# The second batch's keys: pooled by GpSimd and transposed on TensorE, in place of pooling by small matmuls

## The chip, the cores and the metric

The kernel runs on one core of one Trainium2 chip. A core has five engines with a queue each: TensorE (PE, with its weight loads as PEld), VectorE (DVE), ScalarE (ACT), GpSimd (POOL) and SyncE (SP, which here issues transfers). The metric is the time of one execution on the device in microseconds. Before the change it is 291.39 us in the median of 7 runs (290.43 to 291.57).

## What is computed

Attention with pooled keys and values, then a feed-forward layer with the activation h cos h. There are 8 batches, 8 heads, 576 positions and 64 dimensions for each head; keys and values are averaged over groups of 8 positions, so each head has 72 pooled keys.

```python
def _attn_ref(q, k, v):
    B, H, S, D = q.shape            # 8, 8, 576, 64
    pool = 8
    Sp = S // pool                  # 72
    scale = 1.0 / np.sqrt(D)
    k_p = k.reshape(B, H, Sp, pool, D).mean(axis=3)
    v_p = v.reshape(B, H, Sp, pool, D).mean(axis=3)
    scores = scale * np.matmul(q, k_p.transpose(0, 1, 3, 2))
    scores = scores - np.max(scores, axis=-1, keepdims=True)
    attn = np.exp(scores)
    attn = attn / (np.sum(attn, axis=-1, keepdims=True) + 1e-09)
    return np.matmul(attn, v_p)

def _moe_ref(x, w_in, w_out):       # x: 4608 x 512, w_in: 512 x 2048, w_out: 2048 x 512
    h = x @ w_in
    g = h * np.cos(h)
    return g @ w_out
```

All tensors are float32 in memory; the kernel works in bf16 with float32 sums.

## The kernel before

The feed-forward layer is done in 9 tiles of 512 tokens, `t` = 0 to 8; attention is done a batch (576 tokens) at a time. A prologue computes the attention of batch 0. In tile `t` PE first does the **up phase**, eight pairs `fp` of 128-column blocks, each pair 8 matmuls of 128x512 (L317); ACT takes the cosine (L327) and DVE the product (L331). Then comes the **down phase**, into which the attention of batch `t + 1` is woven. Tile 0 does the down phase with 64 plain matmuls of 128x512 (L334), numbered `n` = 0 to 63; later tiles use a scheme of seven half-size products (L395). The order in every queue is the order of the program text: the kernel is scheduled by hand, each engine runs its instructions in that order, and semaphores make an instruction wait for what it needs.

**Tile 0.** Its attention is that of batch 1. Its keys come in an "even" layout, 128 partitions each holding 9 successive positions of a head, so the pooling over 8 positions crosses partitions. `pool_k_mm` (L168) does it on PE: a matmul with a 0/1 matrix `groups` adds the positions and transposes in one step, 36 small matmuls for two pairs of heads. It is called twice after the up pair `fp` = 4, into the banks `obanks`; `put_kk` (L143) copies the sums to `kk[1]` with four copies on DVE and four on ACT. After `fp` = 5 and 6, `q_transpose_mm` (L203) transposes the queries of batch 1 on PE, nine blocks of 128x128 each time.

In the down phase of tile 0 a list `fill` says before which `n` a piece of attention goes: the rest of batch 0 (`scores(t, REST)`, L222), the first scores of batch 1 (`S_(0, 0)`), the pooling of the values by matmuls (`pool_v_mm`, L176), the products with the values (L251, `V_`). The matmuls run over w_out's pieces in the order 0, 2, 1, 3: `n` = 8 is the first that needs piece 2, `n` = 16 piece 1, `n` = 24 piece 3.

**Later batches.** `load_kv` (L114) loads keys or values with 72 partitions, each holding the 8 positions of one pooled key. `pool_add` does the pooling on POOL: four adds of halves (L151), two more (L153), and for keys two (L156) that write the sum twice side by side into `kp2`. `k_transpose` (L182) moves `kp2` to `kk` by a transposing transfer.

**Loads.** POOL issues all loads of tile 0 in one row: q, k and v of batch 0, w_in pieces 0 to 2, the keys of batch 1 (`load_even`, L95), half of its queries, w_in 3, the other queries, w_out 0, the values of batch 1; three memsets (`vz[1]`, `kp2`); w_out 2, 1 and 3 (L128); then keys, queries and values of batch 2. POOL's transfers count on eight semaphores in rotation: an issue waits until the transfer eight places before it has landed. The issue of the values of batch 2 also waits for `pool_v_mm` on PE, whose input it overwrites. Then POOL computes four weight differences (L351) and pools the keys and values of batch 2.

PSUM has three double banks `banks[0..2]` and two single ones, `obanks`. `g1` to `g4` are SBUF tiles for later tiles; before these, g1 and g2 hold scratch with which DVE builds `groups` in the first 4 us, and g3 holds `groups`.

Of the kernel before, what the change touches and what calls it, by code (L numbers as in the profile page):

```python
# [10 lines left out]
BF16 = mybir.dt.bfloat16  # L11
ACTF = mybir.ActivationFunctionType
ADD = mybir.AluOpType.add
SUB = mybir.AluOpType.subtract

POOL = 8
# [4 lines left out]
def kernel(  # L21
# [9 lines left out]
    nc = tc.nc  # L31
    B, H, S, D = q.shape
    Sp = S // POOL
# [37 lines left out]
    g1, g2, g3, g4 = [wpool.tile([128, HF, HT], BF16, name=f"g{i}") for i in range(1, 5)]  # L71
# [4 lines left out]
    kk = [wpool.tile([128, H, SpA], BF16, name=f"kk{i}") for i in range(2)]  # L76
    kp2 = [wpool.tile([SpA, H, 2, D], BF16, name=f"kp2{i}") for i in range(2)]
# [16 lines left out]
    def load_even(dst, b, src, j0=0, j1=KCH):  # L94
        nc.gpsimd.dma_start(out=dst[:, j0:j1].rearrange("p j t d -> p j (t d)"), in_=even_view(src, b, j0, j1))  # L95
# [31 lines left out]
    def load_w_out(cg):  # L127
        nc.gpsimd.dma_start(  # L128
            out=w_out_sb[cg],
            in_=moe_w_out[cg * 512:(cg + 1) * 512, :].rearrange("(f p) m -> p f m", p=128))  # L130
# [14 lines left out]
    def pool_add(b, which):  # L145

        st = staged.pop((which, b))
        x, s = st, half_sums
        add = nc.gpsimd.tensor_tensor
        for h in range(0, H, 2):  # L150
            add(out=s[:, h:h + 2], in0=x[:, h:h + 2, 0:4, :], in1=x[:, h:h + 2, 4:8, :], op=ADD)  # L151
        for h in range(0, H, 4):
            add(out=s[:, h:h + 4, 0:2, :], in0=s[:, h:h + 4, 0:2, :], in1=s[:, h:h + 4, 2:4, :], op=ADD)  # L153
        if which == "k":
            for slot in range(2):
                add(out=kp2[b % 2][:Sp, :, slot, :], in0=s[:, :, 0, :], in1=s[:, :, 1, :], op=ADD)  # L156
        else:
            s = s.rearrange("p (j a) t d -> p j a t d", a=2)
            add(out=v_part(b), in0=s[..., 0, :], in1=s[..., 1, :], op=ADD)
# [12 lines left out]
    def pool_v_mm(b, pair):  # L172
        vb = staged["v", b]
        for t in range(ROW):
            for hp, rows in enumerate(half):
                nc.tensor.matmul(pair[:Sp, hp, 0:KCH * D], lhsT=groups[rows, t, :], rhs=vb[rows, :, t, :],  # L176
                                 start=(t == 0), stop=(t == ROW - 1))
        nc.vector.tensor_copy(out=v_part(b).rearrange("p j a d -> p a j d"),
                              in_=pair[:Sp, :, 0:KCH * D].rearrange("p a (j d) -> p a j d", j=KCH))

    def k_transpose(b):
        nc.sync.dma_start_transpose(out=kk[b % 2], in_=kp2[b % 2].rearrange("p h s d -> p (h s d)"))  # L182
# [290 lines left out]
    q_tile(1)  # L473
    for cg in range(3):
        load_w_in(cg)
    load_even(staged["k", 1], 1, k)
    load_even(staged["q", 1], 1, q, 0, 2)
    load_w_in(3)
    load_even(staged["q", 1], 1, q, 2, 4)
# [2 lines left out]
    nc.gpsimd.memset(vz[1], float(POOL))  # L482
    for i in range(2):
        nc.gpsimd.memset(kp2[i], 0.0)
    for cg in (2, 1, 3):
        load_w_out(cg)

    def warm_up(n, bank):

# [34 lines left out]
    for t in range(NT):  # L524
        b = t + 1
        if t > 0:

            for fp in up_order(t)[0:2]:
                up_mm(t, fp, 0, 2)
        for n, fp in enumerate(up_order(t)):  # L530
            up_mm(t, fp, 2 if n < 2 else 0)
            between = ()
            if t == 0:
                if fp == 4:
                    puts = pool_k_mm(1, obanks[0], 0, 2), pool_k_mm(1, obanks[1], 2, 4)
                elif fp in (5, 6):
                    g0 = 9 * (fp - 5)
                    puts = q_transpose_mm(1, obanks[0], g0, g0 + 5), q_transpose_mm(1, obanks[1], g0 + 5, g0 + 9)
                if fp in (4, 5, 6):
                    puts[0](vec)  # L540
                    between = ((puts[1], act),)
            up_g(t, fp, between)
            if 0 < t and 3 <= n < 6:
                put_gs(*[(k, 0) for k in (((3,), (1,), ()) if t == 1 else ((1, 2), (3,), (4,)))[n - 3]])
            if 0 < t and b < B:
                if n == 0:
                    q_transpose(b)
                elif n == 2:
                    k_transpose(b)
        mms = [(ms, fc) for ms in range(4) for fc in range(FFCH)]  # L550
        if t == 0:
            mms = [(ms, fc) for hm in range(2) for cg in (0, 2, 1, 3) for ms in range(2 * hm, 2 * hm + 2)
                   for fc in range(4 * cg, 4 * cg + 4)]


        def S_(n, bank):
            return lambda: scores(b, us[n], banks[bank])

        later = []

        def V_(n, bank, wait=None):
            return lambda: values(b, us[n], banks[bank], wait)

        fill = []
        if t < B:
            exp_tables()
            fill = [(1, lambda: scores(t, REST, banks[2])), (16, lambda: values(t, REST, banks[1]))]
        if t == 0:
            fill = [(2, fill[0][1]), (2, S_(0, 0)), (8, lambda: pool_v_mm(1, banks[1])),
                    (8, lambda: values(t, REST, banks[2])), (8, S_(1, 0)), (8, V_(0, 1)),  # L570
                    (18, S_(2, 2)), (21, V_(1, 0, later)), (26, S_(3, 1)), (32, lambda: later.pop()()),
                    (32, V_(2, 2)), (40, V_(3, 0))]
        if t < FIRST:
            fi = 0
            for n, (ms, fc) in enumerate(mms):
                while fi < len(fill) and fill[fi][0] <= n:
                    fill[fi][1]()
                    fi += 1
                down_mm(obanks[ms % 2], ms, fc)
                if fc == FFCH - 1:  # L580
                    down_out(t, ms, obanks[ms % 2])
                if n == 4:
                    put_weights(0, nc.vector, (1,))
                elif n == 36:
                    put_weights(1, nc.vector, (3,))
            put_weights(1, nc.vector, (2, 4))
        else:
            products, reads = down_products(t)

            def product(i, j=0, k=2 * HF):  # L590
                for mm in products[i][j:k]:
                    mm()

            us = BY_TOKENS
            later = []

            u0, u1, u2, u3 = [(b, us[i], banks[j]) for i, j in enumerate((2, 1, 0, 1))]
            ur = (t, REST, banks[2])

            def scores_of(*parts):  # L600
                for part in parts:
                    scores_mm(*part)
                for part in parts:
                    scores_exp(*part)

            def muls():
                while later:
                    later.pop(0)()

            steady, rest = b < B, t < B  # L610
            if rest:
                exp_tables()
            product(0)
            product(1, 0, 2)
            if steady:
                scores_of(u0, u1, u2)
            elif rest:
                scores_of(ur)
            product(1, 2)
            if t == 1:  # L620
                put_g(2, 0)
            put_gs((1, 1), (2, 1))
            reads[0]()
            put_g(3, 1)
            reads[1]()
            if t == 1:
                put_g(4, 0)
            if steady:
                values(*u0, later)
            product(2)  # L630
            reads[2]()
            muls()
            if steady:
                values(*u1, later)
            product(3)
            reads[3]()
            muls()
            put_g(4, 1)
            if steady:
                values(*u2, later)  # L640
            product(4)
            reads[4]()
            muls()
            if steady:
                scores_of(ur, u3)
            product(5, 0, 4)
            if rest:
                values(*ur, later)
            product(5, 4, 12)
            muls()  # L650
            if steady:
                values(*u3, later)
            product(5, 12)
            reads[5]()
            muls()
            product(6)
            reads[6]()
        if t < B:
            sin_tables()
        if 0 < t and b + 1 < B:  # L660

            nc.gpsimd.tensor_copy(out=gate, in_=kk[b % 2][0:1, 0, 0:1])
        if b + 1 < B:
            load_kv(b + 1, "k", k)
            load_q(b + 1)
            load_kv(b + 1, "v", v)
            if t == 0:
                put_weights(0, nc.gpsimd, (3, 2, 4))
                put_weights(1, nc.gpsimd, (1,))
            pool_add(b + 1, "k")  # L670
            pool_add(b + 1, "v")
# [28 lines left out]
```

The softmax here doesn't subtract the row's maximum and nothing guards it: scores larger than these inputs give would overflow.

## Time and profile before

| | |
|---|---|
| median of 7 runs | 291.39 us (290.43 to 291.57) |
| the profiled execution | 291.24 us |
| its span, first to last instruction | 289.5 us |
| PE busy | 280.7 us (97%) |
| DVE busy | 233.5 us (81%) |
| ACT busy | 207.9 us (72%) |
| POOL busy | 150.9 us (52%) |
| mean clock granted to PE | 0.997 of full |
| mean of all transfers | 114 GB/s |
| transfers from 20 to 45 us | 204 to 207 GB/s |

The span is what the profiler sees of one execution, so its parts are compared with each other and with the span; the medians of several runs are compared with each other. Busy time is a sum over the whole span; where the change acts, from 7 to 45 us, the timeline of each engine has to be read.

### The profile page before, as it was taken

Reading aid. Unit: us, or ns where it says so; the run is one execution under the profiler, and the core shown is the slowest. Engines: PE = TensorE matmul, PEld = TensorE weight load, DVE = VectorE, ACT = ScalarE, POOL = GpSimd, SP = SyncE. Lnnn points to the kernel's source line nnn. Section 1 sums busy time; section 2 is a strip of 40 time slices with the busy share of each in tenths; the row PEclk is TensorE's granted clock in tenths of the full one; section 3 lists DMA queues with packets and bytes.
Section 4 is the critical chain, followed back from the end, with each engine's and each line's share of the span. In section 5 each row is a group of like instructions: output and inputs, shape, how many; then the busy total and the mean of one; then the engine's idle time right before and its main releaser. Section 6 shows DMA issues by size and latency. Waiting matters only on the chain.

```text
span 289.5 us, 5446 instructions
## 1 busy us (share of the span) xinstructions
PE 280.7 (97%) x2168; PEld 178.0 (62%) x2168; DVE 233.5 (81%) x314; ACT 207.9 (72%) x265; POOL 150.9 (52%) x145
## 2 busy tenths in 40 slices
PE   7889999999999999999999999999999999999994
PEld 2545554446864586458745884588448854884583
DVE  6458747799988989798989897989798979855972
ACT  3786798378887798679966997699759976436600
POOL 8553189995698469836984499439920000000000
PEclk9999999999999999999999999999999999999998
DMA  7999999454939592969185936694670060006014
GB/s 155 203 207 207 206 205 213 111 109 60 174 77 177 72 163 43 204 87 165 24 188 82 176 51 151 106 170 71 146 106 0 5 144 1 2 7 140 0 39 109
DMA packets 44489, 32.97 MB, mean 114 GB/s; under 512 B 22192, under 2 KB 40112, under 8 KB 44464
## 3 DMA queue, kind: packets, MB, share of 16 engines
q0 software_dynamic: 19744, 18.07, 40.0%
q1 hardware_dynamic: 24080, 14.03, 23.6%
q10 hardware_dynamic: 640, 0.52, 0.8%
q8 instruction: 17, 0.28, 0.4%
q14 instruction: 8, 0.07, 0.1%
HBM read 36.70 MB, written 9.44 MB: 159 GB/s over the span
## 4 chain that ended last, share of the span: by engine, by line
PE 67%; DVE 6%; ACT 0%; issue 0%; DVEq 0%
PE obank L395 29%; PE bank L317 26%; PE bank L251 4%; PE obank L317 4%; PE bank L222 2%; DVE g_sb L331 2%; PE bank L395 2%; DVE xT L262 2%; DVE g L361 2%; DVE o_two L411 1%; ACT cos L327 0%; DVE q_sb L411 0%; DVEq L411 0%
## 5 line engine op out<-in xcount | busy, mean ns | idle before, releaser
L317 PE MATMUL bank<-xT,w_in_sb 128*128 128x512 bf16 x512 | 114.0, 379 | 0.1
L327 ACT ACTIVATE cos<-bank,half_pi 128x1024 f32<-128x1024 f32 x64 | 70.3, 1113 | 46.8 <-PE bank L317 46.8
L317 PEld LDWEIGHTS <-w_in_sb 128*128 128x128 bf16 x576 | 56.1, 98 | 66.1 <-issue 0.5
L331 DVE TENSOR_TENSOR g_sb<-bank,cos 128x1024 bf16<-128x1024 f32 x64 | 77.2, 1220 | 21.0 <-ACT cos L327 21.0
L151 POOL TENSOR_TENSOR half_sums<-kv_st 72x512 f32<-72x512 bf16 x48 | 54.3, 1158 | 27.1 <-DMA kv_st<-in_k_dram 26.6
L395 PEld LDWEIGHTS <-g 128*128 128x128 bf16 x512 | 48.9, 98 | 7.2 <-issue 1.4
L262 DVE TENSOR_TENSOR xT<-bank,inv 64x512 bf16<-64x512 f32 (+1 forms) x72 | 45.3, 629 | 6.3 <-ACT inv L258 4.9
L257 ACT ACTIVATE inv<-bank 64x512 f32<-64x512 f32 (+1 forms) x72 | 39.1, 544 | 10.5 <-PE bank L251 9.4
L395 PE MATMUL obank<-w,g 128*128 128x256 bf16 x368 | 43.6, 272 | 0.0
L395 PEld LDWEIGHTS <-g_sb 128*128 128x128 bf16 x384 | 36.8, 98 | 7.8 <-issue 1.2
L229 ACT ACTIVATE ex<-bank 72x1024 bf16<-72x1024 f32 (+1 forms) x40 | 35.0, 928 | 2.0 <-PE bank L222 1.9
L153 POOL TENSOR_TENSOR half_sums<-half_sums 72x512 f32<-72x512 f32 x24 | 32.2, 1359 | 0.0
L395 PE MATMUL obank<-w_out_sb,g_sb 128*128 128x256 bf16 x240 | 28.9, 273 | 0.3 <-DVE g_sb L331 0.3
L361 DVE TENSOR_TENSOR g<-g_sb 128x1024 bf16<-128x1024 bf16 x32 | 23.6, 736 | 0.5
L258 ACT ACTIVATE inv<-inv 128x512 f32<-128x512 f32 (+1 forms) x36 | 21.0, 583 | 1.1
L251 PE MATMUL bank<-ex,vz 72*128 72x256 bf16 (+1 forms) x176 | 20.0, 243 | 0.1
L156 POOL TENSOR_TENSOR kp<-half_sums 72x512 bf16<-72x512 f32 x12 | 16.3, 1374 | 0.5
L251 PEld LDWEIGHTS <-vz 72*128 72x128 bf16 x176 | 13.6, 97 | 3.5 <-DVE xT L262 0.5
L334 PE MATMUL obank<-w_out_sb,g_sb 128*128 128x512 bf16 x64 | 15.3, 379 | 0.4 <-DMA w_out_sb<-in_moe_w_out_dram 0.4
L395 PE MATMUL obank<-w_out_sb,g 128*128 128x256 bf16 x112 | 15.7, 273 | 0.0
L395 PE MATMUL obank<-w,g_sb 128*128 128x256 bf16 x128 | 15.3, 273 | 0.0
L317 PE MATMUL obank<-xT,w_in_sb 128*128 128x512 bf16 x64 | 15.1, 379 | 0.0
(85 smaller groups left out, 246.4 us busy)
## 6 DMA issues: line engine op xcount, KB each, us to landing
out_dram<-o_two SPq DMA_DIRECT2D x64, 128.0 KB, 2.4
kv_st<-in_v_dram POOLq DMA_DIRECT2D x8, 576.0 KB, 12.8
kv_st<-in_k_dram POOLq DMA_DIRECT2D x7, 576.0 KB, 7.7
q_b<-in_q_dram POOLq DMA_DIRECT2D x6, 576.0 KB, 10.0
w_in_sb<-in_moe_w_in_dram POOLq DMA_DIRECT2D x4, 512.0 KB, 14.4
w_out_sb<-in_moe_w_out_dram POOLq DMA_DIRECT2D x4, 512.0 KB, 18.3
q_b<-in_q_dram POOLq DMA_DIRECT2D x4, 288.0 KB, 12.7
g_sb<-in_k_dram SPq DMA_DIRECT2D x1, 576.0 KB, 3.6
```

The lines of the kernel that those rows point to most:

```text
L151: add(out=s[:, h:h + 2], in0=x[:, h:h + 2, 0:4, :], in1=x[:, h:h + 2, 4:8, :], op=ADD)
L153: add(out=s[:, h:h + 4, 0:2, :], in0=s[:, h:h + 4, 0:2, :], in1=s[:, h:h + 4, 2:4, :], op=ADD)
L229: nc.scalar.activation(out=ex[:, 0:nh * n].rearrange("p (a n) -> p a n", a=2), in_=pair[:Sp, :, 0:nh * n // 2], func=ACTF.Exp, scale=scale ...
L251: nc.tensor.matmul(pair[:, hp, (i // 2) * n:(i // 2 + 1) * n], lhsT=vz[b % 2][:, pj, 2 * hp:2 * hp + 2, :].rearrange("p a d -> p (a d)"), ...
L257: nc.scalar.activation(out=inv[half[1 - hp]], in_=pair[half[1 - hp], hp, 0:w], func=ACTF.Ln)
L258: nc.scalar.activation(out=inv, in_=inv, func=ACTF.Exp, scale=-1.0)
L262: nc.vector.tensor_mul(out=x_out(b, u, half[hp]), in0=cols(pair[half[hp], hp, :], u), in1=cols(inv[half[1 - hp]], u))
L317: nc.tensor.matmul(h[j] if h is obanks else h[:, j, :], lhsT=w_in_sb[fc // 4][:, ki, (fc % 4) * 128:(fc % 4 + 1) * 128], rhs=xT[:, ki, t * ...
L327: nc.scalar.activation(out=c, in_=ps, func=ACTF.Sin, bias=half_pi[:, :1])
L331: nc.vector.tensor_mul(out=o, in0=ps, in1=c)
L361: nc.vector.tensor_tensor(out=out[:, f0:f1], in0=x, in1=y, op=op)
L395: mms.append(lambda bank=bank, first=first, g=g, w=w, fc=fc, p=p: nc.tensor.matmul(bank[p], lhsT=g(fc, p), rhs=w(fc), start=(first and fc ...
```

## The change

The keys of batch 1 are no longer loaded in the even layout. They are loaded as later batches are, with 72 partitions, in two halves of four heads into `g1` and `g2`, which are free by then. `pool_add` learns to take its input from two parts. It is called for batch 1 on POOL after the issue of w_out pieces 2 and 1, ahead of piece 3. The two calls of `pool_k_mm` in the up phase of tile 0 and their copies are gone. A new function `k_transpose_mm` transposes the sums on PE, a head at a time, into `banks[2]`, and DVE copies them to `kk[1]` in one instruction; it is called at the end of the up phase, ahead of the first down matmul. The first two entries of `fill` go from `n` = 2 to `n` = 4.

```diff
     def pool_add(b, which):
 
         st = staged.pop((which, b))
-        x, s = st, half_sums
+        parts = st if isinstance(st, list) else [st]
+        s = half_sums
         add = nc.gpsimd.tensor_tensor
         for h in range(0, H, 2):
-            add(out=s[:, h:h + 2], in0=x[:, h:h + 2, 0:4, :], in1=x[:, h:h + 2, 4:8, :], op=ADD)
+            i, h0 = divmod(h, H // len(parts))
+            x = parts[i][:, h0:h0 + 2]
+            add(out=s[:, h:h + 2], in0=x[:, :, 0:4, :], in1=x[:, :, 4:8, :], op=ADD)
...
+    def k_transpose_mm(b, bank):
+        ps = bank.bitcast(BF16)[:, 0:H * Sp].rearrange("p (h n) -> p h n", n=Sp)
+        for h in range(H):
+            nc.tensor.matmul(ps[:, h, :], kp2[b % 2][:Sp, h].rearrange("p s d -> p (s d)"), identity[:Sp, :Sp],
+                             is_transpose=True)
+        nc.vector.tensor_copy(out=kk[b % 2][:, :, 0:Sp], in_=ps)
...
     for cg in range(3):
         load_w_in(cg)
-    load_even(staged["k", 1], 1, k)
+    staged["k", 1] = [x[:Sp].rearrange("p f n -> p (f n)").rearrange("p (h t d) -> p h t d", h=H // 2, t=POOL)
+                      for x in (g1, g2)]
+    for i, x in enumerate(staged["k", 1]):
+        nc.gpsimd.dma_start(out=x.rearrange("p h t d -> p h (t d)"),
+                            in_=k[1, 4 * i:4 * i + 4].rearrange("h (p t) d -> p h (t d)", t=POOL))
     load_even(staged["q", 1], 1, q, 0, 2)
...
-    for cg in (2, 1, 3):
+    for cg in (2, 1):
         load_w_out(cg)
+    pool_add(1, "k")
+    load_w_out(3)
...
             if t == 0:
-                if fp == 4:
-                    puts = pool_k_mm(1, obanks[0], 0, 2), pool_k_mm(1, obanks[1], 2, 4)
-                elif fp in (5, 6):
+                if fp in (5, 6):
                     g0 = 9 * (fp - 5)
                     puts = q_transpose_mm(1, obanks[0], g0, g0 + 5), q_transpose_mm(1, obanks[1], g0 + 5, g0 + 9)
-                if fp in (4, 5, 6):
                     puts[0](vec)
                     between = ((puts[1], act),)
...
         if t == 0:
+            k_transpose_mm(1, banks[2][:, 0, :])
             mms = [(ms, fc) for hm in range(2) for cg in (0, 2, 1, 3) for ms in range(2 * hm, 2 * hm + 2)
                    for fc in range(4 * cg, 4 * cg + 4)]
...
-            fill = [(2, fill[0][1]), (2, S_(0, 0)), (8, lambda: pool_v_mm(1, banks[1])),
+            fill = [(4, fill[0][1]), (4, S_(0, 0)), (8, lambda: pool_v_mm(1, banks[1])),
```

## The prediction

> **What bounds the kernel now.** I read the page first: TensorE (PE) is busy 97% of the 289.5 us span, and the chain that ended last is 67% PE. A PE microsecond won or lost should therefore reach the end, unless a wait stands in its way. All edits lie before 45 us, so I went to the timeline of that stretch, engine by engine. First PE (start us, us, engine, line, operation, shapes, count, idle before and its releaser):
>
> ```profile
> 25.86 1.36 PE L168 MATMUL obank<-g,kv_st 64*64 64x72 bf16 x72
> 27.15 1.90 PE L317 MATMUL bank<-xT,w_in_sb 128*128 128x512 bf16 x8
> 28.89 0.67 PE L203 MATMUL obank<-identity,q_b 128*128 128x128 bf16 x9
> 29.39 1.89 PE L317 MATMUL bank<-xT,w_in_sb 128*128 128x512 bf16 x8
> 31.11 0.67 PE L203 MATMUL obank<-identity,q_b 128*128 128x128 bf16 x9
> 31.62 1.89 PE L317 MATMUL bank<-xT,w_in_sb 128*128 128x512 bf16 x8
> 33.34 0.59 PE L334 MATMUL obank<-w_out_sb,g_sb 128*128 128x512 bf16 x2
> 33.87 0.55 PE L222 MATMUL bank<-qT,kk 64*72 64x64 bf16 x12
> 34.35 1.47 PE L334 MATMUL obank<-w_out_sb,g_sb 128*128 128x512 bf16 x6
> 35.97 1.17 PE L176 MATMUL bank<-kv_st,g 64*72 64x256 bf16 x18
> 38.44 1.89 PE L334 MATMUL obank<-w_out_sb,g_sb 128*128 128x512 bf16 x8
> 40.70 0.59 PE L334 MATMUL obank<-w_out_sb,g_sb 128*128 128x512 bf16 x2 [0.36 <-DMA w_out_sb<-in_moe_w_out_dram]
> ```
>
> The first line is what the change removes: 72 small matmuls, worth 27.15 - 25.86 = 1.29 us from start to next start. The last line matters most: the 17th down matmul (n=16) starts at 40.70 because it waited for the third piece of w_out. PE was there about 0.5 us earlier (38.44 + 8 x 0.2205, the pace of L317 and L334 from start to start, is 40.20). So time won before 40.7 us is not all kept. From 40.70 to the end of this down phase at 53.5 PE shows no idle; a shift of n=16 is a shift of the end.
>
> Then GpSimd (POOL), which gets the new work:
>
> ```profile
> 17.09 0.74 POOL L95 DMA_DIRECT2D kv_st<-in_v_dram  x1 [2.86 <-DMA w_in_sb<-in_moe_w_in_dram]
> 17.82 0.97 POOL L482 MEMSET vz<- 72x1024 bf16 x1
> 18.71 1.86 POOL L484 MEMSET kp<- 80x1024 bf16 x2
> 20.50 0.75 POOL L128 DMA_DIRECT2D w_out_sb<-in_moe_w_out_dram  x1
> 22.21 0.74 POOL L128 DMA_DIRECT2D w_out_sb<-in_moe_w_out_dram  x1 [0.96 <-DMA w_in_sb<-in_moe_w_in_dram]
> 37.44 0.84 POOL L114 DMA_DIRECT2D kv_st<-in_v_dram  x1 [7.61 <-PE bank L176]
> 74.70 4.50 POOL L151 TENSOR_TENSOR half_sums<-kv_st 72x512 f32<-72x512 bf16 x4 [5.18 <-DMA kv_st<-in_k_dram]
> 79.16 2.94 POOL L153 TENSOR_TENSOR half_sums<-half_sums 72x512 f32<-72x512 f32 x2
> 82.18 2.50 POOL L156 TENSOR_TENSOR kp<-half_sums 72x512 bf16<-72x512 f32 x2
> ```
>
> POOL issues its loads over eight semaphores in rotation, so a load waits until the one eight places before it has landed. It is idle 7.61 us before 37.44. The last three lines are one pooling of keys as it stands later in the kernel: the same eight adds that the change puts into the first up phase.
>
> [...]the adds of L153 take 1.26 us at the median, but 1.72 at most. Between 24 and 34 us DVE runs only L331 (one PSUM input) and copies out of PSUM, so I expect the short times. [...]here nine take 29.39 - 28.89 = 0.50 us in a row, 55 ns each, and I use that.[...]
>
> **Part by part.**
>
> *Removed.* 1.29 us of PE at 25.86; four DVE casts (1.26 us) and four ACT casts (1.13 us), which lay beside PE and which no matmul waited for: worth nothing.
>
> *The key load.* It becomes two loads of 72 partitions into g1 and g2, still before q and w_in 3: the same bytes at the same place in the queue. g1 and g2 are free (DVE's last read of them ends at 3.7 us). [...]The landing of each later load is set by its slowest engine: one runs about 1.5 to 2 us late in the trace. [...]the last landing comes some 0.4 us earlier (w_in 3 at 28.8 becomes about 28.2, w_out's third piece at 40.65 about 40.3). If not, up to 0.8 later.
>
> *One load more on the semaphores.* All later issues move back a place in the rotation: v of batch 1 waits for w_in 1 (landed 19.41 by issue plus time to landing) instead of w_in 0. An issue came 0.28 us after its landing for w_out 0, v and w_out 3, so v goes out at 19.69 instead of 17.09, a shift of 2.6. The queue is full until past 40 us (DMA share at its ceiling, 207 GB/s), so transfers don't start later. But POOL's own order does: memsets and two w_out issues follow as before (20.50 - 17.09 = 3.41, then 0.75 and 0.74), giving 19.69 + 3.41 + 1.49 = 24.60 as the start of pooling. Both key halves are there by about 24.
>
> *The pooling.* L151 and L153 run 7.03 us where nothing disturbs them (4.49 + 2.50 and a gap), L156 2.50: 9.53 us. It ends at 24.60 + 9.53 = 34.13. It was hidden in POOL's idle 7.61 us as to POOL; w_out 3 goes out at 34.2 instead of 25.0, still before the queue runs dry, so it costs nothing. Upper bound: the pooling at 46.88 us took 10.88, with DVE's two-input subtractions beside it: end 35.5. Lower bound: the shortest rows with no gaps, 4.49 + 2.49 + 2.50 = 9.48.
>
> *PE's path.* The sixth pair of up matmuls now starts at 25.86 and ends at 27.60; nine transposes to 28.10; then w_in 3, about 0.3 us of wait; two more groups of eight and nine transposes (1.74 + 0.50 + 1.72): the up phase ends at about 32.3 instead of 33.34. The new transposes wait for kp2 there: with about 0.1 us of signal they start at 34.2. PE stands idle 1.9 us, and everything queued behind it on PE, the whole down phase, stands too. Eight transposes at 55 ns are 0.42. Then four down matmuls (0.88) to 35.5. The rest scores reuse the bank that DVE's new copy reads. DVE is free of the last up product at about 34.9 (PE end 32.3 + 0.2 + cosine 1.11 + product 1.23), and the copy of 576 columns costs about 0.45 (128x640 took 0.49)[...]: done at 35.4 to 35.7. So the scores start at 35.5 to 35.7. From there to n=16, by before's intervals: scores 0.48, four matmuls 0.88, pooling of v 1.10, its copy to the first values 0.92, values 0.45, eight matmuls 1.77 = 5.60. n=16 starts at 41.1 to 41.3 instead of 40.70. The wait for w_out is gone; what is late in its place is kp2. Sum: +0.4 to +0.6 us.
>
> *Later.* v of batch 2 is issued after the pooling of v1 on PE, about 0.7 us later, and POOL's weights and poolings with it. POOL waits 2.4 us and more at its gate in later tiles, and kp2 for batch 2 (57.8) is asked for at 60.0: no cost.
>
> Profiled execution: 291.24 us, span 289.5, so 1.7 outside the span; the median of the runs is 291.39, 0.15 above it. I add the change to the median.
>
> **Rivals.**
> - A, likeliest (0.55): PE waits for kp2 as worked out; +0.3 to +1.0, my value +0.6 because small delays on this chain only add: 292.0.
> - B (0.15): POOL is disturbed and pools in 10.9 us: transposes at 35.6, n=16 at 42.5, +1.8: 293.2. For it: the first pooling of the trace took that. Against: no two-input DVE work here.
> - C, not slower (0.25): kp2 is in time. The matmuls removed less the transposes added are 0.87 us of PE, and the last wait is again w_out's third piece, at about 40.3: 0.4 earlier, 291.0; up to 0.9 if w_out comes earlier too. It decides if pooling ends by about 33.3, that is 0.8 earlier than my sum: possible only if the issue of v doesn't wait for w_in 1's slowest engine, or the adds run shorter than any in the trace. Against: every term is a measured row.
> - D (0.05): the idle 1.9 us together with the wait for w_in 3 lets PE's clock fall[...].
>
> **Numbers.** 292.0, range 290.9 to 293.3: A whole, most of B and C. About 0.6 us (0.2%) is what a measurement of this kernel tells from none. A gives 0.25 within and 0.30 slower; B and D 0.20 slower; C 0.13 faster, 0.12 within: faster 0.13, same 0.37, slower 0.50.
>
> **What would show it.** Right: eight adds on POOL from about 24.6 to 34.1; a PE gap of 1.5 to 2.2 us before the new transposes, released by POOL; no wait on w_out at n=16, which starts near 41.2; from there the old distances. Wrong: pooling ends before PE comes (no gap, C); a clock under full after 34 us (D); n=16 waiting for w_out later than 40.7[...]; later stages longer than before.

## The result and the profile after

| | before | changed |
|---|---|---|
| median | 291.3 us (32 runs, 290.31 to 291.9) | 293.12 us (13 runs, 291.66 to 293.83) |
| ratio | | 1.0059, 95% interval 1.0046 to 1.0071 |
| profiled execution, its span | 291.24 us, 289.5 us | 293.83 us, 291.9 us |
| PE busy | 280.7 us | 279.9 us |
| POOL busy | 150.9 us | 161.7 us |

The change makes the kernel 0.59% slower, about 1.7 us. PE does 0.8 us less work and POOL 10.8 us more. The profiled execution of the changed kernel is the slowest of its 13, so its trace shows the losses large. I read it for places and causes, and the medians for sizes.

The timeline of PE in the changed kernel (line numbers are those of the changed file: L327 is the up phase, L213 the query transposes, L187 the new transposes, L344 the down phase, L232 the scores, L179 the pooling of v):

```profile
28.26 0.67 PE L213 MATMUL obank<-identity,q_b 128*128 128x128 bf16 x9
29.57 1.90 PE L327 MATMUL bank<-xT,w_in_sb 128*128 128x512 bf16 x8 [0.64 <-DMA w_in_sb<-in_moe_w_in_dram]
31.31 0.67 PE L213 MATMUL obank<-identity,q_b 128*128 128x128 bf16 x9
31.81 1.89 PE L327 MATMUL bank<-xT,w_in_sb 128*128 128x512 bf16 x8
34.76 0.43 PE L187 MATMUL bank<-identity,kp 72*128 72x72 bf16 x8 [1.06 <-POOL kp L159]
35.02 1.03 PE L344 MATMUL obank<-w_out_sb,g_sb 128*128 128x512 bf16 x4
36.53 0.55 PE L232 MATMUL bank<-qT,kk 64*72 64x64 bf16 x12 [0.47 <-DVE kk L189]
...
40.45 2.32 PE L344 MATMUL obank<-w_out_sb,g_sb 128*128 128x512 bf16 x10
...
45.22 0.59 PE L344 MATMUL obank<-w_out_sb,g_sb 128*128 128x512 bf16 x2 [0.27 <-DMA w_out_sb<-in_moe_w_out_dram]
```

The small matmuls are gone, and four waits stand in the brackets of these lines that weren't there: for w_in 3 (0.64), for GpSimd's sums (1.06), for DVE's copy of the transposed sums (0.47), and, at the 25th down matmul, for w_out's fourth piece (0.27). The wait at the 17th, the one that bound before, is gone: n=16 is the ninth of the ten at 40.45, so it starts near 40.45 + 8 x 0.2205 = 42.2, 1.5 us later than before. The next up phase starts at 55.39 instead of 53.48, 1.9 us later. Half a microsecond more is lost in tile 2, where PE waits 0.29 us for a product of DVE; what set that off was not tried.

Part of the lateness is not the change's. The up phase itself started 0.78 us later, because PE had waited longer for the first queries of batch 0, a load issued ahead of everything that the change touches. Before:

```profile
7.49 0.45 PE L203 MATMUL bank<-identity,q_b 128*128 128x128 bf16 x5 [0.58 <-DMA q_b<-in_q_dram]
...
17.10 8.82 PE L317 MATMUL bank<-xT,w_in_sb 128*128 128x512 bf16 x40
```

and in the changed kernel:

```profile
8.21 0.45 PE L213 MATMUL bank<-identity,q_b 128*128 128x128 bf16 x5 [1.33 <-DMA q_b<-in_q_dram]
...
17.88 10.55 PE L327 MATMUL bank<-xT,w_in_sb 128*128 128x512 bf16 x48
```

In the thirteen traces used here this start lies between 16.78 and 17.88 us, and the changed kernel's is the latest. So times of one execution are not sizes of the change.

The timeline of POOL in the changed kernel:

```profile
19.32 0.74 POOL L95 DMA_DIRECT2D kv_st<-in_v_dram  x1 [1.78 <-DMA w_in_sb<-in_moe_w_in_dram]
...
22.97 0.74 POOL L128 DMA_DIRECT2D w_out_sb<-in_moe_w_out_dram  x1 [0.17 <-issue]
24.43 0.74 POOL L128 DMA_DIRECT2D w_out_sb<-in_moe_w_out_dram  x1 [0.72 <-DMA g<-in_k_dram]
25.19 4.49 POOL L154 TENSOR_TENSOR half_sums<-g 72x512 f32<-72x512 bf16 x4
29.65 2.48 POOL L156 TENSOR_TENSOR half_sums<-half_sums 72x512 f32<-72x512 f32 x2
32.21 2.49 POOL L159 TENSOR_TENSOR kp<-half_sums 72x512 bf16<-72x512 f32 x2
34.65 0.78 POOL L128 DMA_DIRECT2D w_out_sb<-in_moe_w_out_dram  x1
```

The pooling takes 32.21 + 2.49 - 25.19 = 9.51 us, as in the undisturbed rows of the trace before. It starts 0.6 us later than forecast, because the issue ahead of it waits until the first key half has landed.

And DVE at the hand-over, where L341 is the product of the last up pair and L189 the new copy:

```profile
34.88 1.22 DVE L341 TENSOR_TENSOR g_sb<-bank,cos 128x1024 bf16<-128x1024 f32 x1 [1.01 <-ACT cos L337]
36.02 0.45 DVE L189 COPY kk<-bank 128x576 bf16<-128x576 bf16 x1
```

The transposes were done at about 35.0; the copy began a microsecond later, when DVE had finished the product. PE had come late to that last pair because of w_in 3, and the copy inherited it.

The loads themselves, each by its issue plus its time to landing: w_in 3 landed at 11.34 + 18.2 = 29.5 us (before: 9.16 + 19.6 = 28.8), w_out's third piece at 24.43 + 17.0 = 41.4 (40.6), its fourth at 34.65 + 10.5 = 45.2 (43.1). The sixteen landing records of w_in 3 stand in two groups now: eight between 26.0 and 26.8, eight between 27.5 and 29.5. Before, fifteen stood between 26.2 and 27.4 and one at 28.8. These too are the times of one slow execution; how they vary is told with the runs on the loads.

### The profile page after: what moved, and what is told of

The parts are those of the page before. It is cut to its first block, busy times and chain, and to the rows that moved or that the text cites. A ratio compares the mean times of both kernels' runs of the same rounds, so it can differ in the third digit from the quotient of the medians.

```text
span 291.9 us, 5324 instructions
## 1 busy us (share of the span) xinstructions
PE 279.9 (96%) x2104; PEld 176.9 (61%) x2104; DVE 233.0 (80%) x311; ACT 206.6 (71%) x261; POOL 161.7 (55%) x154
## 4 chain that ended last, share of the span: by engine, by line
PE 69%; DVE 3%; ACT 0%; issue 0%
PE obank L405 31%; PE bank L327 27%; PE bank L261 4%; PE obank L327 4%; PE bank L232 3%; DVE g_sb L341 2%; PE bank L405 2%; DVE g L371 1%; ACT cos L337 0%; DVE o_two L421 0%
## 5 line engine op out<-in xcount | busy, mean ns | idle before, releaser
L327 PE MATMUL bank<-xT,w_in_sb 128*128 128x512 bf16 x512 | 113.9, 379 | 0.9 <-DMA w_in_sb<-in_moe_w_in_dram 0.6
L327 PEld LDWEIGHTS <-w_in_sb 128*128 128x128 bf16 x576 | 56.2, 98 | 67.3 <-issue 1.2
L341 DVE TENSOR_TENSOR g_sb<-bank,cos 128x1024 bf16<-128x1024 f32 x64 | 77.1, 1219 | 21.0 <-ACT cos L337 20.9
L154 POOL TENSOR_TENSOR half_sums<-kv_st 72x512 f32<-72x512 bf16 x48 | 55.3, 1179 | 28.1 <-DMA kv_st<-in_k_dram 27.6
L267 ACT ACTIVATE inv<-bank 64x512 f32<-64x512 f32 (+1 forms) x72 | 39.2, 544 | 11.8 <-PE bank L261 10.8
L156 POOL TENSOR_TENSOR half_sums<-half_sums 72x512 f32<-72x512 f32 x26 | 34.2, 1332 | 0.0
L371 DVE TENSOR_TENSOR g<-g_sb 128x1024 bf16<-128x1024 bf16 x32 | 23.0, 720 | 0.5
L159 POOL TENSOR_TENSOR kp<-half_sums 72x512 bf16<-72x512 f32 x14 | 18.6, 1350 | 0.5
L344 PE MATMUL obank<-w_out_sb,g_sb 128*128 128x512 bf16 x64 | 15.3, 379 | 0.3 <-DMA w_out_sb<-in_moe_w_out_dram 0.3
L327 PE MATMUL obank<-xT,w_in_sb 128*128 128x512 bf16 x64 | 15.1, 379 | 0.0
```

The lines of the kernel that those rows point to most:

```text
L154: add(out=s[:, h:h + 2], in0=x[:, :, 0:4, :], in1=x[:, :, 4:8, :], op=ADD)
L267: nc.scalar.activation(out=inv[half[1 - hp]], in_=pair[half[1 - hp], hp, 0:w], func=ACTF.Ln)
L327: nc.tensor.matmul(h[j] if h is obanks else h[:, j, :], lhsT=w_in_sb[fc // 4][:, ki, (fc % 4) * 128:(fc % 4 + 1) * 128], rhs=xT[:, ki, t * ...
L341: nc.vector.tensor_mul(out=o, in0=ps, in1=c)
L371: nc.vector.tensor_tensor(out=out[:, f0:f1], in0=x, in1=y, op=op)
```

## Experiments: what the scores wait for

Theory 1, formed on these lines: the late weights and the copy behind the late product set the time. Theory 2, that of the forecast: GpSimd's sums set it. A ratio is always to the kernel before on the same chip; its 95% interval stands in parentheses.

**The copy on ScalarE.**

```diff
-        nc.vector.tensor_copy(out=kk[b % 2][:, :, 0:Sp], in_=ps)
+        nc.scalar.copy(out=kk[b % 2][:, :, 0:Sp], in_=ps)
```

> The changed kernel, with the copy of the transposed sums on ScalarE instead of VectorE. Theory 1: the rest scores waited for that copy, which stood on VectorE behind the last up product (free at 36.10 us in its profile), and the sums of GpSimd alone would have let them start at 35.9: scores at about 35.9 instead of 36.53, the whole kernel about 0.6 us faster than the changed one, near 292.5. Theory 2: only GpSimd's end (34.70) counts: no change, 293.1.

Measured: 293.31 us, ratio 1.0069 (1.0046 to 1.0093): no gain. Its PE timeline shows where the gain went:

```profile
34.55 0.43 PE L187 MATMUL bank<-identity,kp 72*128 72x72 bf16 x8 [0.85 <-POOL kp L159]
...
35.78 0.55 PE L232 MATMUL bank<-qT,kk 64*72 64x64 bf16 x12
...
45.16 0.59 PE L344 MATMUL obank<-w_out_sb,g_sb 128*128 128x512 bf16 x2 [0.92 <-DMA w_out_sb<-in_moe_w_out_dram]
```

The scores do start 0.75 us sooner, at 35.78, as theory 1 said of the place. But the 25th down matmul starts at 45.16, where it started at 45.22: its wait for w_out's fourth piece grew from 0.27 to 0.92 and took the gain. Theory 1 was right about the copy and wrong that this was the end of the row.

**No wait for the sums.** The transposes read the other, zeroed buffer, so the keys of batch 1 count as zero; GpSimd still pools.

```diff
-            nc.tensor.matmul(ps[:, h, :], kp2[b % 2][:Sp, h].rearrange("p s d -> p (s d)"), identity[:Sp, :Sp],
+            nc.tensor.matmul(ps[:, h, :], kp2[(b + 1) % 2][:Sp, h].rearrange("p s d -> p (s d)"), identity[:Sp, :Sp],
```

> The changed kernel, with the transposes reading the other, zeroed sum buffer: GpSimd still pools, but TensorE does not wait for it (the keys of batch 1 count as zero, so attention of batch 1 is left without its scores). Theory 1: the copy behind the last product still holds the scores until 36.5: no gain, 293.0 to 293.1. Theory 2: the wait of 1.06 us goes and nothing takes its place: about 292.0.

Measured: 292.82 us, ratio 1.0060 (1.0036 to 1.0083): no gain that can be told from none, against theory 2. In its PE timeline the wait has moved to the copy:

```profile
32.39 0.42 PE L187 MATMUL bank<-identity,kp 72*128 72x72 bf16 x8
...
35.38 0.55 PE L232 MATMUL bank<-qT,kk 64*72 64x64 bf16 x12 [1.70 <-DVE kk L189]
```

**Both at once.**

> Both edits at once: copy on ScalarE and transposes from the zeroed buffer (attention of batch 1 without its scores). Theory 1: scores at about 35.5, 1.0 us less than the changed kernel, near 292.1; more than the two edits alone bring together. What stays above the kernel before is then the loads. Theory 2: as with the wait alone taken away, 292.0.

Measured: 292.94 us, ratio 1.0052 (1.0029 to 1.0075). Neither theory's 292.0 to 292.1. Its PE timeline:

```profile
34.83 0.55 PE L232 MATMUL bank<-qT,kk 64*72 64x64 bf16 x12 [0.60 <-ACT kk L189]
...
40.90 0.59 PE L344 MATMUL obank<-w_out_sb,g_sb 128*128 128x512 bf16 x2 [0.26 <-DMA w_out_sb<-in_moe_w_out_dram]
```

The scores start 1.7 us sooner than in the changed kernel. Now the 17th matmul waits for w_out's third piece again. This profiled execution took 292.05 us, at the good end of its seven runs (median 292.94); in the slower ones the weights may have come later still, which no trace shows. Sums, copy and weights stand one behind the other; taking away the first two leaves a time that can't be told from the changed kernel's.

## Experiments: the loads

**The key loads of the change alone,** in the kernel before; the small matmuls pool the keys of batch 0.

```diff
-    load_even(staged["k", 1], 1, k)
+    for i, x in enumerate((g1, g2)):
+        x = x[:Sp].rearrange("p f n -> p (f n)").rearrange("p (h t d) -> p h t d", h=H // 2, t=POOL)
+        nc.gpsimd.dma_start(out=x.rearrange("p h t d -> p h (t d)"),
+                            in_=k[1, 4 * i:4 * i + 4].rearrange("h (p t) d -> p h (t d)", t=POOL))
...
-        kb = staged["k", b]
+        kb = staged["k", 0]
```

> The kernel before, with only the key load of the change: two loads of 72 partitions into g1 and g2, which nothing reads; the small matmuls pool the keys of batch 0 once more. Theory 1: [...]w_in 3 lands at about 29.5 instead of 28.8 and w_out's third piece at about 41.4 instead of 40.65; the 17th down matmul starts at about 41.45: +0.7 us, near 292.0. Theory 2: the same bytes in the same place in the queue cost nothing: 291.3.

Measured: 292.37 us, ratio 1.0033 (1.0020 to 1.0047). There is no pooling of these keys on GpSimd, no new transpose, no new wait for sums, and more than half of the loss is there. Its PE timeline has the waits for weights, at n=16 and n=24:

```profile
41.05 0.59 PE L334 MATMUL obank<-w_out_sb,g_sb 128*128 128x512 bf16 x2 [0.27 <-DMA w_out_sb<-in_moe_w_out_dram]
...
44.85 0.59 PE L334 MATMUL obank<-w_out_sb,g_sb 128*128 128x512 bf16 x2 [1.02 <-DMA w_out_sb<-in_moe_w_out_dram]
```

The fourth piece was issued here at 25.42 and landed at 25.42 + 19.4 = 44.8. So a late issue is not needed to make it late.

**Two loads in the old layout:** only one load more, and every later issue one place back in the rotation.

```diff
-    load_even(staged["k", 1], 1, k)
+    load_even(staged["k", 1], 1, k, 0, 2)
+    load_even(staged["k", 1], 1, k, 2, 4)
```

> The kernel before, with its key load of 128 partitions cut into two loads of two pairs of heads: only the extra load and the shift of every later issue by one place in the rotation. Theory 1[...]: 291.3, no change. The third possibility (the extra place costs): about 292.3, as with the key loads of the change alone.

Measured: 291.42 us, ratio 1.0015 (1.0004 to 1.0027), close to theory 1, by which an even layout costs nothing, and far from 292.3, with an interval just above no change.

**Two loads cut by partitions, 64 and 8, alone,** read by nobody, into a part of xT (`k1_st`) that is free until later.

```diff
-    load_even(staged["k", 1], 1, k)
...
+    for p0, p1 in ((0, 64), (64, Sp)):
+        nc.gpsimd.dma_start(out=k1_st[p0:p1].rearrange("p h t d -> p h (t d)"),
+                            in_=k[1].rearrange("h (p t) d -> p h (t d)", t=POOL)[p0:p1])
```

> The kernel before with only the key loads, cut by partitions (64 and 8) and read by nobody; the small matmuls pool the keys of batch 0 once more. [...]291.2 to 291.6, as with two even loads. If any load of these pieces costs: about 292.3.

Measured: 292.08 us, ratio 1.0020 (1.0005 to 1.0035), between its two expectations, of which the first takes the cut by heads for the cause. The profiled execution is one of its slowest (292.91). There the weights are as late as with the keys cut by heads, with waits at n=16 and n=24:

```profile
40.97 0.59 PE L334 MATMUL obank<-w_out_sb,g_sb 128*128 128x512 bf16 x2 [0.66 <-DMA w_out_sb<-in_moe_w_out_dram]
...
44.73 0.59 PE L334 MATMUL obank<-w_out_sb,g_sb 128*128 128x512 bf16 x2 [0.99 <-DMA w_out_sb<-in_moe_w_out_dram]
```

**One load of 72 partitions,** in the changed kernel, into the same part of xT; the rotation is then that of the kernel before.

> The changed kernel, with its keys in one load of 72 partitions: the rotation of semaphores is that of the kernel before[...]. Theory 1: weights land as late as with two loads[...]: 292.5 to 293.3. A third possibility, that the extra place in the rotation is what costs: w_in 3 lands as before the change and the time falls below 292.3.

Measured: 292.74 us, ratio 1.0066 (1.0040 to 1.0091): the old rotation brings nothing back. In its trace the sums bind and not the weights: the one load lands whole at 24.9, GpSimd waits 2.84 us for it, and PE then waits 1.47 us for the sums.

What follows: the loads cost by themselves. A load more costs some 0.15% (0.04 to 0.27). The layout of 72 partitions cut by heads stands higher (1.0033) than the two even loads (1.0015) and the cut into 64 and 8 (1.0020), but the intervals overlap.

The landings point the same way without proving it. With the keys cut by heads, w_in 3 landed anywhere between 28.4 and 29.5 us in six traces, and w_out's third piece between 40.3 and 41.4. But w_in 1, which stands ahead of the keys in the queue, itself landed between 18.1 and 19.0 there. Counted from its landing, each load taken at its last landing record, they are steadier:

| from w_in 1's landing to that of | w_in 3 | w_out's third piece | w_out's fourth piece |
|---|---|---|---|
| even layout (before; two even loads) | 9.4 us, 9.4 | 21.2, 21.4 | 23.7, 23.8 |
| keys cut by heads (six traces) | 10.0 to 10.5 | 21.9 to 22.4 | 24.9 to 26.1 |
| one load of 72 partitions | 10.3 | 22.2 | 25.2 |
| keys cut into 64 and 8 (four) | 9.1 to 10.5 | 21.4 to 22.4 | 23.9 to 26.2 |

So the keys cut by heads delay w_in 3 by 0.6 to 1.1 us. With the loads alone, whose fourth issue is early, the fourth piece follows after 26.0, no sooner than with the late issue. Why stays open: no trace shows how a load is shared out among the transfer engines. One candidate that no run separates is the count of packets: between 20 and 22.9 us the queue moved 722 packets at 192 GB/s in the changed kernel and 759 at 202 GB/s with its loads alone, but 540 at 207 GB/s before.

## Experiments: filling the gap

**The cut by partitions in the changed kernel.**

> The changed kernel, with its two key loads cut by partitions, 64 and 8, with all heads each, instead of by heads: the same count of loads and the same bytes[...]. (They go into a part of xT that is free until later tiles.) Theory 1, [...]w_in 3 back at 28.9 or before, w_out's fourth piece at 43 to 43.5 instead of 45.0, no wait ahead of the 25th down matmul; what is left is the wait for sums and copy: about 292.1. Theory 2, GpSimd's sums set the time: within 0.3 us of the changed kernel, 293.

Measured: 293.76 us, ratio 1.0093 (1.0066 to 1.0121). It was to repair the late weights and brought no gain; its ratio stands above the changed kernel's 1.0059 (1.0046 to 1.0071), with overlapping intervals. First its PE timeline, then PE's clock, from the table of busy time by stage (for each stretch: its length, busy time and count of each engine, PEclk as a share of full, the share of busy transfer engines, GB/s):

```profile
34.56 0.66 PE L187 MATMUL bank<-identity,kp 72*128 72x72 bf16 x8 [2.43 <-DVE g_sb L341]
35.03 1.90 PE L344 MATMUL obank<-w_out_sb,g_sb 128*128 128x512 bf16 x4
```

```profile
33.00:34.00 1.00, 0.00 (x0) 0.00 (x0) 0.69 (x1) 0.98 (x2) 1.00 (x2) 1.00 1.21 204
34.00:35.00 1.00, 0.44 (x8) 0.44 (x9) 0.54 (x1) 0.58 (x1) 1.00 (x2) 0.60 1.25 208
35.00:36.00 1.00, 1.00 (x7) 0.45 (x5) 0.74 (x2) 0.00 (x0) 1.00 (x2) 0.50 1.24 206
36.00:37.00 1.00, 1.00 (x7) 0.16 (x7) 0.32 (x1) 0.00 (x0) 0.84 (x2) 0.50 1.24 205
37.00:38.00 1.00, 1.00 (x14) 0.50 (x13) 0.00 (x0) 0.64 (x2) 0.00 (x0) 0.69 1.25 209
```

w_in 3 landed early enough here that PE did not wait for it. So PE came to the transposes sooner and stood idle 2.43 us (the bracket names the product of DVE; GpSimd's adds ended at 34.50, just before, and are what released it). After 2.1 us of that gap PE's clock fell to half, from 34.2 to 37.6 us (the shares 0.60, 0.50, 0.50 and 0.69): four down matmuls took 1.90 us where they took 1.03.

**The same, with PE kept busy** by nine matmuls on constants, which nobody reads:

```diff
+            warm_up(9, banks[2][:, 1, :])
             k_transpose_mm(1, banks[2][:, 0, :])
```

> The key loads cut by partitions (64 and 8) as before, with nine idle matmuls of 128x512 on TensorE between the last up matmul and the transposes, so that it is not idle while it waits. In the run without them the clock of TensorE stood at half from 34.4 to 37.8 us. If that is why the cut loads brought no gain: clock full throughout, 1.5 to 1.8 us less than with the cut alone, near 292.1 and below the changed kernel. If the gap is not the cause: 293.8 as before.

Measured: 292.27 us, ratio 1.0043 (1.0027 to 1.0060), 1.5 us below the run without them (1.0066 to 1.0121). Its PE timeline:

```profile
32.35 2.10 PE L507 MATMUL bank<-g 128*128 128x512 bf16 x9
34.67 0.43 PE L187 MATMUL bank<-identity,kp 72*128 72x72 bf16 x8 [0.21 <-POOL kp L159]
34.94 1.03 PE L344 MATMUL obank<-w_out_sb,g_sb 128*128 128x512 bf16 x4
```

The transposes start no sooner; the clock stays full. So the idle gap costs more than its own length, and between these two traces the clock is the difference. The other executions limit this: only four of the six without the matmuls have a mean clock that tells of such a fall (0.991 to 0.994, with times of 293.13 to 295.25 us). The other two (0.997 and 0.999) took 292.91 and 293.44, still above 292.27. How much of the 1.5 us is the clock is therefore not settled.

**Useful work in the gap.** Four down matmuls ahead of the transposes, four behind, the copy on ScalarE ahead of its table load (1.28 us in the traces of both kernels). The line that places them:

```diff
-            fill = [(4, fill[0][1]), (4, S_(0, 0)), (8, lambda: pool_v_mm(1, banks[1])),
+            fill = [(4, lambda: (k_transpose_mm(1, banks[2][:, 0, :]), exp_tables())), (8, fill[0][1]), (8, S_(0, 0)), (8, lambda: pool_v_mm(1, banks[1])),
```

> The changed kernel with four down matmuls ahead of the transposes and four behind, ahead of the rest scores, and the copy on ScalarE, ahead of its table load: TensorE has work while GpSimd pools. If the wait for the sums is what costs beside the loads: the gap of about 1 us shrinks to 0.3 or less, the 17th down matmul comes near 41.0 and the kernel about 0.9 us ahead of the changed one, near 292.2; what stays is the late weights. If only the late weights count (theory 1 alone): no change, 293.

Measured: 292.2 us, ratio 1.0039 (1.0023 to 1.0055). Its PE timeline:

```profile
32.47 1.02 PE L344 MATMUL obank<-w_out_sb,g_sb 128*128 128x512 bf16 x4
33.47 0.43 PE L187 MATMUL bank<-identity,kp 72*128 72x72 bf16 x8
...
40.31 0.59 PE L344 MATMUL obank<-w_out_sb,g_sb 128*128 128x512 bf16 x2 [0.18 <-DMA w_out_sb<-in_moe_w_out_dram]
...
43.59 0.59 PE L344 MATMUL obank<-w_out_sb,g_sb 128*128 128x512 bf16 x2 [0.51 <-DMA w_out_sb<-in_moe_w_out_dram]
```

The wait for the sums is gone, and the two waits in these lines are for weights. (Between the transposes and these two PE also waits 0.52 us for an exponential of ScalarE.) Its ratio is near that of the key loads alone (1.0033). Against the changed kernel it is some 0.2% better, with intervals that overlap.

**The pooling also ahead of the issue of w_out's third piece.**

> As the run before, with the pooling also moved ahead of the issue of w_out's third piece on GpSimd, so that it starts at the landing of the first key half (about 24.4, ends about 34.0). Expected: no wait of TensorE for the sums; 291.5 to 292.2, the rest of the distance to the kernel before being late weights, which this leaves as they are; w_out's third piece is issued at 34 us, and if it then lands after 41.4 the gain is lost again (293).

Measured: 293.27 us, ratio 1.0074 (1.0056 to 1.0093), slower than the run before. The execution that was profiled took more than twice the time of the others, so its trace isn't used, and whether the late issue of the third piece is the reason was only argued.

**Both repairs:** later transposes and the cut by partitions.

> Both repairs: transposes behind four down matmuls with the copy on ScalarE, and the key loads cut by partitions (64 and 8). If the change's cost is the sum of late weights and the wait for the sums: below the later transposes alone (292.2), 291.4 to 291.9, at the kernel before. If the sums now bound because the cut load lands whole only at 24.9: 292.2 again.

Measured: 292.52 us, ratio 1.0040 (1.0025 to 1.0054). The second repair adds nothing to the first: the larger key load lands at 24.1 us there, where the first half of the keys cut by heads had landed at 22.9 in the run with the later transposes alone, and PE waits 1.13 us for the sums again. None of the versions beat the kernel before.

## Why the forecast was right, and what it sized wrongly

The direction and the range held: 292.0 was forecast, 290.9 to 293.3, and 293.12 was measured. The change cost 1.8 us by the medians where the forecast had 0.6. That the number fell within the range is in part luck: the upper end takes in rival B, slow adds on GpSimd, which did not come about; late weights filled that room, where the forecast had them slightly early. The wait that it named is in the trace, but it is one of several that stand close together, and not the one that alone sets the time.

- *What is removed and added on PE*: right. Busy time fell by 0.8 us (0.87 forecast), and the removed matmuls bought nothing. Eight transposes took 35.02 - 34.76 = 0.26 us, not 0.42, which was eight times the 55 ns of a 128x128 one.
- *The pooling on GpSimd*: right in length (9.51 against 9.53 us), 0.6 late in its start. The forecast let the third w_out issue go out at 23.85 without a wait; it waited for the first key half until 24.43.
- *The wait for the sums*: right in place (the sums ended at 34.70, the transposes started at 34.76), 1.06 us instead of 1.9, because PE itself came later, having waited for w_in 3. It was not the whole reason: taken away alone it brought no measurable gain, since the copy stood behind it; with both taken away there was still none, and in that trace PE waited for weights.
- *The copy*: 0.45 us as forecast, but its product ended at 36.1 us, not 34.9, as the up phase ended 1.2 us later than forecast.
- *The key load*: the term that was mis-sized, with the wrong sign. The forecast put w_in 3 at 28.2 and w_out's third piece at 40.3; the other case, up to 0.8 later, stood in the text and got no weight. Both sizes were my estimate, and no trace shows what it rested on. In the trace they landed at 29.5 and 41.4. Two of the six traces with these loads did show 28.4 and 40.3, but in executions whose whole queue ran early: counted from w_in 1, the forecast had w_in 3 after 28.2 - 19.4 = 8.8 us, and all six have it after 10.0 to 10.5, which is the case that got no weight. The loads alone, with nothing else of the change, cost 0.33% (0.20 to 0.47), about 1 us.
- *The later issue of w_out's fourth piece*: forecast at no cost, and none is shown. In the trace the piece landed 2 us later and PE waited for it, but with the loads alone it landed at 44.8 with its early issue too.
- *Rival D*, the clock: it did not happen in the changed kernel, whose gap was 1.06 us and whose mean clock was 0.997 or more in all 13 runs. It did happen when the keys were cut by partitions and the gap grew to 2.43 us. The pair of runs without and with matmuls in the gap differs by 1.5 us, not all of it surely the clock.
- *Rivals B and C* did not come about: the adds were undisturbed, and the sums were not in time. What B stood for is in the trace before: two adds of L153 at 62.30 took 2.94 us, beside an operation of DVE from SBUF (L361) that took 1.77 us instead of the median 0.68; at 89.21, with no such operation beside them, two took 2.50.

In the trace with the gap of 2.43 us the clock fell 2.1 us into it, and the half pace then lasted 3.4 us. In the traces, gaps of 1.06 us in the changed kernel and of 1.70 us without the wait for the sums were not followed by it. A threshold does not come out of these runs, since two of the six executions with the longer gap seem to have kept the full clock.

## What to carry over

When a transfer queue is full (198 to 208 GB/s from 20 to 45 us in the changed kernel) and the next stages run as their weights land, a load of the same bytes is not the same load: in another layout and in two pieces it moved the landing of the weights behind it by 0.6 us and more. The last of a load's landing records is the one that counts: eight of w_in 3's sixteen stood by 26.8 us, the last at 29.5, and PE started at 29.57. One trace doesn't size such a shift, since the whole queue can be early or late by as much; count from a landing that the change cannot reach, and time many runs. Where several waits end within a microsecond of each other, removing any one shows the next; find them all in the trace before pricing one. An idle gap of TensorE can cost more than its length (after 2.1 us of one of 2.43 the clock stood at half for 3.4 us), so reaching a wait sooner need not help; filling the gap with constant matmuls did (292.27 us against 293.76).

## What was not expected

A repair that let TensorE arrive earlier brought no gain, and in four of its six runs the clock's mean tells of a fall: 293.76 us with the gap, 292.27 us with constant matmuls in it. And the loads of one piece of data moved landings 15 us and more behind them: counted from w_in 1, w_out's fourth piece, the last of the weights in the queue, came 1.1 to 2.4 us later in the six traces with the keys cut by heads than in the two with the even layout.
